# Float64 words converted in two parts in a three-layer float32 kernel: the last sum of a conversion issued with the next one

## The chip, the cores and the metric

The kernel runs on one core of a Trainium2 chip. The metric is the device time of one execution in microseconds (us); the kernel before takes 1666.84 us (median of three executions, 1666.79 to 1670.42). Engines: PE is TensorE (matmul), PEld its weight loads, DVE VectorE, ACT ScalarE, POOL GpSimd, SP the sync engine, whose queue issues most DMA transfers.

## The reference

The core of it, with batch 8, 8 heads, sequence 576, head size 64, 32 pack rows, d_model 512 and d_ff 2048:

```
p_packed = sm_attn(p, k, v)             # softmax attention, 32 rows per head
out = sm_attn(q, p_packed, p_packed)    # 576 rows per head
x = out.transpose(0, 2, 1, 3).reshape(4608, 512)
h = x @ moe_w_in;  x = (h * cos(h)) @ moe_w_out
h = x @ moe2_w_in; g = P(h) / (Q(h) + 1e-6); out = g @ moe2_w_out
```

All is float32, but the four weight matrices arrive as float64 (their scale factors make them so): each weight is two 32-bit words, and the kernel turns the words into float32 itself.

## The kernel before

Every product of the two layers is made of three float32r matmuls of split values (hi and lo parts, the function split, L66 and L67), so PE has three passes for each.

**Conversion of the words.** A tile `st` of 128 x 512 x 2 words (512 KB) is loaded; tiles of the tag st64 have three buffers. assemble does, on one tile: ACT scales the low words in place (L80); DVE shifts the high words (L82), puts sign and exponent together (L87) and cuts out the exponent (L90); POOL multiplies the low part by it (L91), which ends the use of `st`; DVE adds the two (L94). cvf and cvp are its two scratch tiles, with two buffers each. For w_out and the second layer's weights convert then makes hi on ACT (L99) and lo on POOL (L100). There are 16 conversions of moe_w_in (only the sum, into w1i), 16 of moe_w_out and 32 of the second layer's weights.

**Stage 1** (about 0 to 140 us): a loop over 16 pairs of batch and half of the heads computes the packed attention: scores (s), Exp, transposes (et), values (pv), the masked and scaled result ppm (DVE, L257), its transpose (pt). One conversion is issued by conv_next in each turn, and the load of the words three conversions on. From the fifth turn, units of the product of packed values and w_in are made (wunit: PE `w`, evacuated by ACT at L298 or DVE at L296 into wev, and written to HBM, L299).

**Stage 2** (about 140 to 840 us): 128 slots, each with mm_h (PE `h`, L532), a chain that makes g = h cos(h) (chain1: ACT u L557, DVE r L558, ACT Abs L562 and Sin L563, DVE g L564, then gh and gl by split) and mm_y of an earlier slot (PE `y`, L581). In the first nine slots `h` has one buffer, and fill puts wunits between. wq tiles are loaded from HBM (L459) and split (L66, L67). Conversions 17 to 32 are issued in the first eight slots; from slot 16 on, each three slots load (load_w2), convert (conv_w2) and write out (L478, L479) one tile of the second layer's weights.

**Stage 3** (the rest): the second layer, mm_h2, chain2 and mm_o.

The program is written in this order, but a scheduler of the language reorders each engine's instructions by its own estimate when it builds the kernel. hold only ties an instruction behind a given matmul in that order. Each engine then runs its list strictly in order.

Of the kernel before, what the change touches and what calls it, by code (L numbers as in the profile page):

```python
# [9 lines left out]
F32 = mybir.dt.float32  # L10
F32R = mybir.dt.float32r
U32 = mybir.dt.uint32
AF = mybir.ActivationFunctionType
ALU = mybir.AluOpType
# [6 lines left out]
def pack_attention_moe_moe_kernel(  # L21
# [14 lines left out]
    nc = tc.nc  # L36
# [5 lines left out]
    NG = B * G  # L42
    C = S // 32
    HS = S // 2
    NFC = DFF // 128
# [8 lines left out]
    def hold(ins, until):  # L54
        if until is None:
            return
        tc.add_manual_dep(
            ins.ins,
            until.ins.name,
            mybir.DependencyInfo(mybir.DependencyClass.NoSync, mybir.DependencyReason.SCHED_ONLY),  # L60
            reason="issue order",
        )
# [8 lines left out]
    def words(w):  # L71
        return w.bitcast(U32).rearrange("p (n t) -> p n t", t=2)

    def assemble(out, wd64, pool, n, until=None):
        up, dn = wd64[:, :, 1], wd64[:, :, 0]
        f = pool.tile([128, n], U32, tag="cvf", bufs=2, name="cvf")
        pw = pool.tile([128, n], U32, tag="cvp", bufs=2, name="cvp")
        dl = dn.bitcast(F32)
        ff, pf = f.bitcast(F32), pw.bitcast(F32)
        hold(nc.scalar.activation(out=dl, in_=dn, func=AF.Copy, scale=2.0 ** -52), until)  # L80
        hold(
            nc.vector.tensor_scalar(  # L82
                out=f, in0=up, scalar1=3, scalar2=0x3FFFFFFF, op0=ALU.logical_shift_left, op1=ALU.bitwise_and
            ),
            until,
        )
        nc.vector.scalar_tensor_tensor(  # L87
            out=f, in0=up, scalar=0xC0000000, in1=f, op0=ALU.bitwise_and, op1=ALU.bitwise_or
        )
        nc.vector.tensor_scalar(out=pw, in0=f, scalar1=0xFF800000, scalar2=None, op0=ALU.bitwise_and)  # L90
        nc.gpsimd.tensor_tensor(out=pf, in0=dl, in1=pf, op=ALU.mult)  # L91
        if out is None:
            out = ff
        nc.vector.tensor_tensor(out=out, in0=ff, in1=pf, op=ALU.add)  # L94
        return out

    def convert(hi, lo, wd64, pool, n, until=None):
        ff = assemble(None, wd64, pool, n, until)
        nc.scalar.activation(out=hi, in_=ff, func=AF.Copy)  # L99
        nc.gpsimd.tensor_tensor(out=lo, in0=ff, in1=hi.bitcast(F32), op=ALU.subtract)  # L100

    const = ctx.enter_context(tc.tile_pool(name="const", bufs=1))
    dram = ctx.enter_context(tc.tile_pool(name="scratch", bufs=1, space=DRAM))
# [5 lines left out]
    w2d = [dram.tile([2 * NFC, 128, 512], F32, name=f"w2d{i}") for i in range(2)]  # L109
# [9 lines left out]
    if True:  # L119
# [4 lines left out]
        cv_p = ctx.enter_context(tc.tile_pool(name="cv", bufs=1, side="right"))  # L124
# [24 lines left out]
        def load_kv(n):  # L149
# [10 lines left out]
            out=coef[:, 4:6], in0=par[:, 4:6], scalar1=-1.0, scalar2=None, op0=ALU.mult  # L160
# [16 lines left out]
        for n0, n1 in ((0, 2), (2, NG)):  # L177
            for h in range(4):
                nc.vector.transpose(
                    out=pbd[32 * h:32 * h + 32, n0:n1, :, h],  # L180
                    in_=px[32 * h:32 * h + 32, n0:n1].rearrange("p n (e i) -> p n e i", e=NDB),
# [28 lines left out]
        def s1(n):  # L210
            ps = ps0.tile([128, 2, 512], F32, tag="s1", bufs=2, name="s1")
            scores(ps, pbd[:, n].rearrange("p e h m -> p e (h m)"), kT_t.pop(n))
            mx = wk.tile([128, 1], F32, tag="mx", bufs=2, name="mx")
            nc.vector.tensor_reduce(out=mx, in_=ps[:, :, 0:HS], op=ALU.max, axis=AX.XY)
            nb = wk.tile([128, 1], F32, tag="nb", bufs=2, name="nb")
            nc.vector.tensor_scalar(out=nb, in0=mx, scalar1=-scale, scalar2=None, op0=ALU.mult)
            E = wk.tile([128, 6, 96], F32, tag="E", bufs=2, name="E")
            sm = wk.tile([128, 1], F32, tag="sm", bufs=2, name="sm")
            nc.scalar.activation(
                out=E.rearrange("p (t r) x -> p t (r x)", t=2),  # L220
                in_=ps[:, :, 0:HS], func=AF.Exp, scale=scale, bias=nb, accum_out=sm,
            )
            rd = wk.tile([128, 1], F32, tag="rd", bufs=3, name="rd")
            nc.vector.tensor_scalar(out=sm, in0=sm, scalar1=1e-9, scalar2=None, op0=ALU.add)
            nc.vector.reciprocal(out=rd, in_=sm)
            E_t[n], rd_t[n] = E, rd
# [134 lines left out]
        st_t = {}  # L361
# [10 lines left out]
        cv1 = [(fq, hp) for fq in range(NQ) for hp in range(NKD)]  # L372
        w1i_t, w1o_s = {}, {}
# [5 lines left out]
        def conv_w1i(x):  # L379
            fq, hp = cv1[x]  # L380
            if hp == 0:
                pool, tag, bufs = (wi_p, "w1i", 2) if fq < 2 else (wb_p, "wb", 8)
                w1i_t[fq] = pool.tile([128, NKD, 512], F32, tag=tag, bufs=bufs, name="w1i")
            assemble(w1i_t[fq][:, hp], st_t.pop(("i", x)), cv_p, 512)

        def load_w1o(f):
            load_st(f, words(w1o[128 * f:128 * f + 128, :]), nc.sync)
# [1 line left out]
        def conv_w1o(f):  # L389
            if f % 4 == 0:  # L390
                w1o_s[f // 4] = [wb_p.tile([128, 4, DM], F32R, tag="wb", bufs=8, name="w1o") for x in range(2)]
            hi, lo = w1o_s[f // 4]
            convert(hi[:, f % 4], lo[:, f % 4], st_t.pop(f), cv_p, 512)


        cvs = [(load_w1i, conv_w1i, x) for x in range(len(cv1))]
        cvs += [(load_w1o, conv_w1o, f) for f in range(NFC)]
        at_cv = [0]

        def conv_next():  # L400
            i = at_cv[0]
            at_cv[0] += 1
            if i < len(cvs):
                cvs[i][1](cvs[i][2])
            if i + 3 < len(cvs):
                cvs[i + 3][0](cvs[i + 3][2])

        prep(0)
        for i in range(3):
# [6 lines left out]
        done0 = [0]  # L416
        s1(0)
        prep(1)
        for n in range(NG + 1):
            if n >= 3:  # L420
                next(at, 1)
            if n + 1 < NG:
                s1(n + 1)
            if n + 3 < NG:
                load_k(n + 3)
            if n + 2 < NG:
                load_v(n + 2)
                prep(n + 2)
            if n < NG:
                et(n)  # L430
            if n >= 1:
                pv(n - 1)
            if n < len(cv1):
                conv_next()
            if n >= 1:
                ppt(n - 1)
            while n >= 5 and done0[0] + 1 < at_cv[0] and (n >= NG or done0[0] < 2 * (n - 4)):
                ps = ps0.tile([128, 2, 512], F32, tag="s1", bufs=2, name="w")
                for i in range(2):
                    fq, hp = cv1[done0[0]]  # L440
                    wunit(0, fq, hp, ps[:, i], False, nc.scalar)
                    done0[0] += 1
# [19 lines left out]
        def split_wq(b, j, eng, until=None):  # L462
            t = wq_t[b, j]
            split(t[:, :, 0, :], t[:, :, 1, :], t[:, :, 1, :].bitcast(F32), eng, until)
# [7 lines left out]
            hold(load_st(("w2", i), src, nc.sync), last_h[0])  # L472

        def conv_w2(i):
            hi = at_p.tile([128, 512], F32R, tag="cvh", bufs=1, name="cvh")
            lo = at_p.tile([128, 512], F32R, tag="cvl", bufs=1, name="cvl")
            convert(hi, lo, st_t.pop(("w2", i)), cv_p, 512, last_h[0])
            nc.sync.dma_start(out=w2d[0][i], in_=hi.bitcast(F32))  # L478
            nc.sync.dma_start(out=w2d[1][i], in_=lo.bitcast(F32))  # L479


        NB = NT // 512
# [38 lines left out]
        last_h = [None]  # L521
# [88 lines left out]
        def slot(n):  # L610
            nonlocal at
            b, hf, j = slots[n]
            s = hf * 8 + j
            mm_h(n)
            chain1(n)
            fill(2)
            if n >= 2:
                mm_y(n - 2)
            else:
                fill(2)  # L620
            fill(1)
            i2, ph2 = divmod(n - 16, 3)
            if 0 <= i2 < 2 * NFC:
                if ph2 == 0:
                    load_w2(i2)
                elif ph2 == 2:
                    conv_w2(i2)
            if b + 1 < B:
                if s == (0 if b else LATE):
                    at = attn2_steps(b + 1, at_p, h_tile, {"aT": ("qT", 1)}, lambda: last_h[0])  # L630
                if s % 2 == 1 if b else s >= LATE:
                    next(at, 1)
                if s == 15:
                    for _ in at:
                        pass
                for jj, (sl, ss) in enumerate(((2, 7), (10, 13), (12, 15), (14, 16))):
                    if s == sl:
                        load_wq(b + 1, jj)
                    if s == ss:
                        split_wq(b + 1, jj, nc.vector, last_h[0])  # L640
            if b > 0 and s == 0:
                split_wq(b, 3, nc.vector, last_h[0])
            move_in(n)
# [20 lines left out]
        for n in range(len(slots)):  # L664
            if n == LATE:
                fill(len(units))
                e0.close()
                at_p = e1t.enter_context(tc.tile_pool(name="at", bufs=1, side="right", **RW))
# [151 lines left out]
```

## Time and profile before

| what | value |
|---|---|
| time, median of 3 | 1666.84 us |
| time of the profiled execution | 1671.62 us |
| its span | 1669.4 us |
| PE busy in the span | 1588.6 us (95%) |
| DVE busy | 1310.0 us (78%) |
| ACT busy | 1190.8 us (71%) |
| POOL busy | 162.1 us (10%) |

The shares are means over stages with different limits, so the stages are read one by one. The 2.2 us between span and time lie around the instructions. Idle time of PE inside the span is what a change of order can win; PE's own work is the same in every order.

### The profile page before, as it was taken

How to read it: one execution, taken by the hardware profiler on the slowest of the kernel's cores; microseconds unless marked ns; L12 is line 12 of the kernel's file. 1: busy time of each engine (PE TensorE's matmuls, PEld its weight loads, DVE VectorE, ACT ScalarE, POOL GpSimd, SP SyncE). 2: the span in 40 equal slices, each digit the busy share in tenths (PEclk: the TensorE clock that was granted, in tenths of full speed). 3: DMA queues.
4: the chain of work that ended last, by engine and by line, in shares of the span. 5: the costliest groups of instructions: out<-in, count | busy, mean ns of one | idle time of the engine just before them, and what ended most of it. 6: DMA issues, size and time to landing. Idle time of an engine off the chain costs nothing.

```text
span 1669.4 us, 24912 instructions
## 1 busy us (share of the span) xinstructions
PE 1588.6 (95%) x9344; PEld 1367.7 (82%) x9344; DVE 1310.0 (78%) x2030; ACT 1190.8 (71%) x1925; POOL 162.1 (10%) x124
## 2 busy tenths in 40 slices
PE   5877999999999999999999999999999999999996
PEld 3554668999999999999998888888888888888884
DVE  7798647787878797868468888888888888888884
ACT  3357656686768686867667878777777777787874
POOL 3135300111121121211000000000000000000000
PEclk9799999999999999999999999999999999999998
DMA  9998452444444453445392201010101001020100
GB/s 281 283 318 279 154 196 88 138 141 138 136 152 141 136 162 122 143 128 160 99 310 77 65 12 53 24 51 26 51 26 44 33 13 64 1 76 1 47 5 26
DMA packets 104376, 183.56 MB, mean 110 GB/s; under 512 B 12096, under 2 KB 46912, under 8 KB 104256
## 3 DMA queue, kind: packets, MB, share of 16 engines
q1 hardware_dynamic: 97344, 167.29, 31.7%
q10 hardware_dynamic: 6912, 14.68, 2.7%
q8 instruction: 74, 1.21, 0.3%
q14 instruction: 46, 0.38, 0.1%
HBM read 117.97 MB, written 63.96 MB: 109 GB/s over the span
## 4 chain that ended last, share of the span: by engine, by line
PE 80%; DVE 6%; ACT 4%; issue 1%; DMA 1%; POOL 0%; SPq 0%; ACTq 0%; DVEq 0%; POOLq 0%
PE h L700 24%; PE o L758 23%; PE y L581 19%; PE h L532 10%; PE w L288 2%; PE s L200 2%; DVE g L564 1%; DVE r L558 1%; DVE gl L67 1%; ACT r L562 1%; DVE wq L67 1%; ACT r L563 1%; ACT L563 0%; DVE sT L350 0%; ACT u L557 0%
## 5 line engine op out<-in xcount | busy, mean ns | idle before, releaser
L581 PE MATMUL y<-gh,w1o 128*128 128x288 f32 x2048 | 438.8, 300 | 2.9 <-DVE yl L67 2.7
L700 PE MATMUL h<-x,w 128*128 128x512 f32 x1728 | 422.2, 393 | 0.0
L700 PEld LDWEIGHTS h<-x,w 128*128 128x128 f32 x1728 | 324.2, 188 | 74.2
L581 PEld LDWEIGHTS y<-gh,w1o 128*128 128x128 f32 x2048 | 338.1, 190 | 10.2 <-issue 5.3
L758 PE MATMUL o<-w,g2h 128*128 128x512 f32 x1152 | 332.9, 393 | 1.2 <-ACT g2h L718 1.2
L581 PE MATMUL y<-gl,w1o 128*128 128x288 f32 x1024 | 300.4, 299 | 2.6 <-DVE gl L67 2.4
L758 PEld LDWEIGHTS o<-w,g2h 128*128 128x128 f32 x1152 | 216.1, 188 | 51.1 <-ACT g2h L718 2.1
L532 PE MATMUL h<-ah,wq 128*128 128x288 f32 x1024 | 231.2, 301 | 11.6 <-DVE g L564 6.1
L581 PEld LDWEIGHTS y<-gl,w1o 128*128 128x128 f32 x1024 | 194.7, 190 | 6.7 <-DVE gl L67 4.2
L758 PE MATMUL o<-w,g2l 128*128 128x512 f32 x576 | 199.9, 393 | 0.0
L733 ACT ACTIVATE sq<-h 128x512 f32<-128x512 f32 x144 | 87.1, 605 | 155.7 <-PE h L700 155.6
L532 PEld LDWEIGHTS h<-ah,wq 128*128 128x128 f32 x1024 | 171.7, 189 | 19.7 <-issue 9.2
L735 DVE SCALAR_TENSOR_TENSOR ab<-sq,coef,ab 128x512 f32<-128x512 f32 x144 | 108.1, 751 | 66.7 <-ACT ab L734 66.5
L557 ACT ACTIVATE u<-h,coef 128x576 f32<-128x576 f32 x128 | 94.3, 737 | 90.1 <-PE h L532 89.6
L532 PE MATMUL h<-al,wq 128*128 128x288 f32 x512 | 151.2, 295 | 0.0
L564 DVE SCALAR_TENSOR_TENSOR g<-h,r 128x576 f32<-128x576 f32 x128 | 96.1, 753 | 59.3 <-ACT r L563 58.6
L91 POOL TENSOR_TENSOR cvp<-st,cvp 128x512 f32<-128x512 f32 x64 | 89.8, 1404 | 502.9 <-DVE cvp L90 233.9
L744 DVE SCALAR_TENSOR_TENSOR ab<-ab,y 128x512 f32<-128x512 f32 x144 | 99.4, 691 | 48.3 <-ACT y L741 48.3
L558 DVE SCALAR_TENSOR_TENSOR r<-u,h 128x576 f32<-128x576 f32 x128 | 95.3, 747 | 52.2 <-ACT u L557 51.7
L758 PEld LDWEIGHTS o<-w,g2l 128*128 128x128 f32 x576 | 108.2, 188 | 24.7
L67 DVE TENSOR_TENSOR gl<-g,gh 128x576 fp32r<-128x576 f32 x128 | 103.3, 809 | 22.3 <-ACT gh L66 21.2
L736 ACT ACTIVATE c<-h,coef 128x512 f32<-128x512 f32 x144 | 113.7, 789 | 8.7 <-DVE g2l L724 8.7
(86 smaller groups left out, 2394.1 us busy)
## 6 DMA issues: line engine op xcount, KB each, us to landing
x<-yd SPq DMA_DIRECT2D x36, 512.0 KB
w<-w2d SPq DMA_DIRECT2D x68, 256.0 KB
st<-in_moe_w_out_dram SPq DMA_DIRECT2D x32, 512.0 KB
wq<-wd SPq DMA_DIRECT2D x64, 256.0 KB
wd<-wev SPq DMA_DIRECT2D x48, 256.0 KB
kx<-in_k_dram SPq DMA_DIRECT2D x16, 576.0 KB
vx<-in_v_dram SPq DMA_DIRECT2D x48, 192.0 KB
qx<-in_q_dram SPq DMA_DIRECT2D x16, 576.0 KB
```

Source lines behind the costliest of these rows:

```text
L67: lo_eng.tensor_tensor(out=lo, in0=src, in1=hi.bitcast(F32), op=ALU.subtract)
L91: nc.gpsimd.tensor_tensor(out=pf, in0=dl, in1=pf, op=ALU.mult)
L532: last_h[0] = nc.tensor.matmul(out=ps[:, u, 0:HS], lhsT=wq[:, g, a, o:o + 128], rhs=a_t[b, g][c][:, hf * HS:hf * HS + HS], start=(i == 0), ...
L557: nc.scalar.activation(out=u, in_=ph, func=AF.Identity, bias=coef[:, 6:7])
L558: nc.vector.scalar_tensor_tensor(out=r, in0=u, scalar=RND, in1=ph, op0=ALU.subtract, op1=ALU.subtract)
L564: nc.vector.scalar_tensor_tensor(out=gt, in0=ph, scalar=2.0 * math.pi, in1=r, op0=ALU.mult, op1=ALU.mult)
L581: nc.tensor.matmul(out=y_t[d][:, 0:HS], lhsT=w1o_s[f // 4][a][:, f % 4, 128 * d:128 * d + 128], rhs=gs[c][:, u], start=(f == 0 and i == 0) ...
L700: nc.tensor.matmul(out=ps, lhsT=w2_s[f][:, 0, a, 128 * kk:128 * kk + 128], rhs=x_t[t, c, kk], start=(i == 0), stop=(i == 3 * NKD - 1),)
L735: nc.vector.scalar_tensor_tensor(out=ab, in0=sq, scalar=coef[:, 5:6], in1=ab, op0=ALU.mult, op1=ALU.add)
L736: nc.scalar.activation(out=c1, in_=ph, func=AF.Identity, scale=coef[:, 3:4], bias=coef[:, 2:3])
L744: nc.vector.scalar_tensor_tensor(out=ab, in0=ab, scalar=QC, in1=y0, op0=ALU.add, op1=ALU.mult)
L758: nc.tensor.matmul(out=o_t[s], lhsT=g2_t[n][a][:, 128 * s:128 * s + 128], rhs=w2_s[f][:, 1, c], start=(f == 0 and i == 0), stop=(f == NFC ...
```

## The change

assemble and convert become words_in (all up to the product on POOL) and words_out (DVE's sum, then hi and lo). conv_next issues words_in of conversion i, then words_out of conversion i - 1, then the load of the words of conversion i + 2 (before: i + 3). In stage 1 it is called in the seventeenth turn as well. conv_w2 leaves its words_out to the next slot with a load, right behind that load. The number of instructions of each kind is the same on every engine. The core of the diff:

```diff
-    def assemble(out, wd64, pool, n, until=None):
+    def words_in(wd64, pool, n, until=None):
...
-        nc.gpsimd.tensor_tensor(out=pf, in0=dl, in1=pf, op=ALU.mult)
-        if out is None:
-            out = ff
-        nc.vector.tensor_tensor(out=out, in0=ff, in1=pf, op=ALU.add)
-        return out
-
-    def convert(hi, lo, wd64, pool, n, until=None):
-        ff = assemble(None, wd64, pool, n, until)
-        nc.scalar.activation(out=hi, in_=ff, func=AF.Copy)
-        nc.gpsimd.tensor_tensor(out=lo, in0=ff, in1=hi.bitcast(F32), op=ALU.subtract)
+        nc.gpsimd.tensor_tensor(out=pw.bitcast(F32), in0=dl, in1=pw.bitcast(F32), op=ALU.mult)
+        return f.bitcast(F32), pw.bitcast(F32)
+
+    def words_out(fp, out=None, hi=None, lo=None, until=None):
+        f, pf = fp
+        out = f if out is None else out
+        hold(nc.vector.tensor_tensor(out=out, in0=f, in1=pf, op=ALU.add), until)
+        if hi is not None:
+            nc.scalar.activation(out=hi, in_=out, func=AF.Copy)
+            nc.gpsimd.tensor_tensor(out=lo, in0=out, in1=hi.bitcast(F32), op=ALU.subtract)
...
+        rest = [None]
+
         def conv_next():
             i = at_cv[0]
             at_cv[0] += 1
-            if i < len(cvs):
-                cvs[i][1](cvs[i][2])
-            if i + 3 < len(cvs):
-                cvs[i + 3][0](cvs[i + 3][2])
+            last, rest[0] = rest[0], cvs[i][1](cvs[i][2]) if i < len(cvs) else None
+            if last is not None:
+                last()
+            if 0 < i < len(cvs) - 2:
+                cvs[i + 2][0](cvs[i + 2][2])
...
-            if n < len(cv1):
-                conv_next()
+            conv_next()
...
-            while n >= 5 and done0[0] + 1 < at_cv[0] and (n >= NG or done0[0] < 2 * (n - 4)):
+            while n >= 5 and done0[0] + 2 < at_cv[0] and (n >= NG or done0[0] < 2 * (n - 4)):
...
+            if 0 < i2 <= 2 * NFC and ph2 == 0:
+                rest[0]()
```

What it moves, at three places on DVE. (In the changed file L82 is L81, L87 is L86, L90 is L89, L94 is L96, L296 is L295, L558 is L566, L564 is L572; cvf<-st is the start of a conversion, cvp its exponent, cvf<-cvf,cvp its sum.)

Place one, DVE around the first split of a wq tile in stage 2, from the 24th conversion's start to the first slot's r; before:

```order
L82 TENSOR_SCALAR cvf<-st_1690 128x512
L87 SCALAR_TENSOR_TENSOR cvf<-st_1690,cvf 128x512
L90 TENSOR_SCALAR cvp<-cvf 128x512
L94 TENSOR_TENSOR cvf<-cvf,cvp 128x512
L296 TENSOR_SCALAR wev<-w 128x512
L94 TENSOR_TENSOR cvf<-cvf,cvp 128x512
L67 TENSOR_TENSOR wq<-wq 128x2x512
L82 TENSOR_SCALAR cvf<-st_1702 128x512
L87 SCALAR_TENSOR_TENSOR cvf<-st_1702,cvf 128x512
L67 TENSOR_TENSOR wq<-wq 128x2x512
L90 TENSOR_SCALAR cvp<-cvf 128x512
L558 SCALAR_TENSOR_TENSOR r<-u,h 128x576
```

And the same stretch now:

```order
L81 TENSOR_SCALAR cvf<-st_1697 128x512
L86 SCALAR_TENSOR_TENSOR cvf<-st_1697,cvf 128x512
L89 TENSOR_SCALAR cvp<-cvf 128x512
L81 TENSOR_SCALAR cvf<-st_1709 128x512
L295 TENSOR_SCALAR wev<-w 128x512
L86 SCALAR_TENSOR_TENSOR cvf<-st_1709,cvf 128x512
L67 TENSOR_TENSOR wq<-wq 128x2x512
L96 TENSOR_TENSOR cvf<-cvf,cvp 128x512
L89 TENSOR_SCALAR cvp<-cvf 128x512
L67 TENSOR_TENSOR wq<-wq 128x2x512
L96 TENSOR_TENSOR cvf<-cvf,cvp 128x512
L566 SCALAR_TENSOR_TENSOR r<-u,h 128x576
```

The 24th conversion's sum goes from ahead of the first wq split to behind it, the start of the 25th comes ahead of the split in its place, and the 25th's sum now stands ahead of r. (The 23rd's sum, fourth above, is just ahead of the stretch now.)

Place two, DVE in the second slot, at the 27th conversion; before:

```order
L82 TENSOR_SCALAR cvf<-st_1807 128x512
L87 SCALAR_TENSOR_TENSOR cvf<-st_1807,cvf 128x512
L94 TENSOR_TENSOR cvf<-cvf,cvp 128x512
L90 TENSOR_SCALAR cvp<-cvf 128x512
L564 SCALAR_TENSOR_TENSOR g<-h,r 128x576
L94 TENSOR_TENSOR cvf<-cvf,cvp 128x512
```

And now:

```order
L86 SCALAR_TENSOR_TENSOR cvf<-st_1816,cvf 128x512
L89 TENSOR_SCALAR cvp<-cvf 128x512
L96 TENSOR_TENSOR cvf<-cvf,cvp 128x512
L572 SCALAR_TENSOR_TENSOR g<-h,r 128x576
L96 TENSOR_TENSOR cvf<-cvf,cvp 128x512
```

Two instructions instead of one stand between the 27th's exponent and its sum.

Place three, DVE in the third slot, from a wq split to g; before:

```order
L67 TENSOR_TENSOR wq<-wq 128x2x512
L87 SCALAR_TENSOR_TENSOR cvf<-st_1897,cvf 128x512
L558 SCALAR_TENSOR_TENSOR r<-u,h 128x576
L90 TENSOR_SCALAR cvp<-cvf 128x512
L82 TENSOR_SCALAR cvf<-st_1909 128x512
L87 SCALAR_TENSOR_TENSOR cvf<-st_1909,cvf 128x512
L296 TENSOR_SCALAR wev<-w 128x512
L90 TENSOR_SCALAR cvp<-cvf 128x512
L94 TENSOR_TENSOR cvf<-cvf,cvp 128x512
L564 SCALAR_TENSOR_TENSOR g<-h,r 128x576
```

And now:

```order
L67 TENSOR_TENSOR wq<-wq 128x2x512
L86 SCALAR_TENSOR_TENSOR cvf<-st_1904,cvf 128x512
L81 TENSOR_SCALAR cvf<-st_1916 128x512
L89 TENSOR_SCALAR cvp<-cvf 128x512
L566 SCALAR_TENSOR_TENSOR r<-u,h 128x576
L86 SCALAR_TENSOR_TENSOR cvf<-st_1916,cvf 128x512
L89 TENSOR_SCALAR cvp<-cvf 128x512
L96 TENSOR_TENSOR cvf<-cvf,cvp 128x512
L295 TENSOR_SCALAR wev<-w 128x512
L572 SCALAR_TENSOR_TENSOR g<-h,r 128x576
```

The evacuation wev<-w now stands behind an exponent and a sum that stood behind it.

## Rows read from the trace of the kernel before

**Rows 1.** The page: span, and busy time by engine.

```profile
span 1669.4 us, 24912 instructions
PE 1588.6 (95%) x9344; PEld 1367.7 (82%) x9344; DVE 1310.0 (78%) x2030; ACT 1190.8 (71%) x1925; POOL 162.1 (10%) x124
```

**Rows 2.** Busy time of each engine by stretch; first the columns.

```profile
core 0: us, PE busy (x) PEld busy (x) DVE busy (x) ACT busy (x) POOL busy (x), PEclk, DMA share, GB/s
104.00:180.00 76.00, 61.83 (x529) 39.87 (x530) 67.67 (x110) 51.12 (x91) 37.05 (x27) 0.96 0.87 279
180.00:300.00 120.00, 112.15 (x664) 95.02 (x663) 73.03 (x103) 74.49 (x117) 10.98 (x9) 0.97 0.43 142
300.00:800.00 500.00, 491.81 (x3600) 482.96 (x3599) 398.38 (x600) 365.47 (x554) 88.62 (x62) 1.00 0.44 139
800.00:1669.00 869.00, 853.24 (x3875) 703.74 (x3873) 687.96 (x1048) 662.89 (x1096) 0.00 (x0) 0.99 0.16 53
```

**Rows 3.** Timeline of PE: start, duration, instruction, [idle before <-what ended it].

```profile
146.70 0.53 PE L532 MATMUL h<-ah,wq 128*128 128x288 f32 x2 [1.22 <-DVE wq L67]
...
154.28 1.12 PE L288 MATMUL w<-w1i,wl 128*128 128x512 f32 x2 [2.70 <-ACT wev L298]
...
172.62 3.24 PE L288 MATMUL w<-w1i,wl 128*128 128x512 f32 x4 [2.18 <-DVE wev L296]
...
190.75 1.88 PE L288 MATMUL w<-w1i,wl 128*128 128x512 f32 x4
```

**Rows 4.** Who waited for whom, 110 to 290 us: total us, times, longest.

```profile
DVE cvf L94 <- POOL cvp L91: 6.3, 9, 1.2
```

**Rows 5.** Timeline of DVE, 136 to 173 us.

```profile
136.78 0.41 DVE L82 TENSOR_SCALAR cvf<-st 128x512 uint32<-128x512 uint32 x1
137.23 1.79 DVE L87 SCALAR_TENSOR_TENSOR cvf<-st,cvf 128x512 uint32<-128x512 uint32 x1
...
143.77 1.74 DVE L94 TENSOR_TENSOR cvf<-cvf,cvp 128x512 f32<-128x512 f32 x1 [0.59 <-POOL cvp L91]
145.43 1.21 DVE L67 TENSOR_TENSOR wq<-wq 128x1024 fp32r<-128x1024 f32 x1
...
148.11 0.69 DVE L87 SCALAR_TENSOR_TENSOR cvf<-st,cvf 128x512 uint32<-128x512 uint32 x1
...
149.86 0.42 DVE L90 TENSOR_SCALAR cvp<-cvf 128x512 uint32<-128x512 uint32 x1
...
151.73 0.69 DVE L94 TENSOR_TENSOR cvf<-cvf,cvp 128x512 f32<-128x512 f32 x1 [0.79 <-POOL cvp L91]
...
161.65 0.75 DVE L564 SCALAR_TENSOR_TENSOR g<-h,r 128x576 f32<-128x576 f32 x1
163.31 1.77 DVE L94 TENSOR_TENSOR cvf<-cvf,cvp 128x512 f32<-128x512 f32 x1 [0.90 <-POOL cvp L91]
...
171.88 0.68 DVE L296 TENSOR_SCALAR wev<-w 128x512 f32<-128x512 f32 x1
```

**Rows 6.** Timeline of POOL, 137 to 152 us.

```profile
137.21 1.27 POOL L100 TENSOR_TENSOR w1o<-cvf,w1o 128x512 fp32r<-128x512 f32 x1 [1.29 <-DVE cvf L82]
...
143.69 1.27 POOL L100 TENSOR_TENSOR w1o<-cvf,w1o 128x512 fp32r<-128x512 f32 x1
...
150.41 1.29 POOL L91 TENSOR_TENSOR cvp<-st,cvp 128x512 f32<-128x512 f32 x1 [2.62 <-issue]
```

**Rows 7.** Timeline of ACT at the first wq split of stage 2.

```profile
141.97 1.06 ACT L66 ACTIVATE wq<-wq 128x1024 fp32r<-128x1024 f32 x1 [0.69 <-DMA wq<-wd]
```

**Rows 8.** Waits of SP's DMA queue, 100 to 180 us.

```profile
SPq L368 <- POOL cvp L91: 20.2, 9, 5.5
```

**Rows 9.** Who waited for whom, 290 to 800 us.

```profile
PE h L532 <- DVE g L564: 5.2, 9, 1.1
...
PE y L581 <- DVE gl L67: 2.4, 4, 1.0
...
DVE cvf L94 <- POOL cvp L91: 2.4, 5, 0.8
```

More of the change, by code (lines that the diff above doesn't have):

```diff
@@ L78, in assemble @@
         dl = dn.bitcast(F32)
-        ff, pf = f.bitcast(F32), pw.bitcast(F32)
         hold(nc.scalar.activation(out=dl, in_=dn, func=AF.Copy, scale=2.0 ** -52), until)
@@ L383, in conv_w1i @@
                 w1i_t[fq] = pool.tile([128, NKD, 512], F32, tag=tag, bufs=bufs, name="w1i")
-            assemble(w1i_t[fq][:, hp], st_t.pop(("i", x)), cv_p, 512)
+            fp = words_in(st_t.pop(("i", x)), cv_p, 512)
+            return lambda: words_out(fp, out=w1i_t[fq][:, hp])
         def load_w1o(f):
@@ L392, in conv_w1o @@
             hi, lo = w1o_s[f // 4]
-            convert(hi[:, f % 4], lo[:, f % 4], st_t.pop(f), cv_p, 512)
+            fp = words_in(st_t.pop(f), cv_p, 512)
+            return lambda: words_out(fp, hi=hi[:, f % 4], lo=lo[:, f % 4])
         cvs = [(load_w1i, conv_w1i, x) for x in range(len(cv1))]
@@ L474, in conv_w2, with fin @@
         def conv_w2(i):
[L475 to L479, printed above, removed]
+            fp = words_in(st_t.pop(("w2", i)), cv_p, 512, last_h[0])
+            def fin():
+                hi = at_p.tile([128, 512], F32R, tag="cvh", bufs=1, name="cvh")
+                lo = at_p.tile([128, 512], F32R, tag="cvl", bufs=1, name="cvl")
+                words_out(fp, hi=hi, lo=lo, until=last_h[0])
+                nc.sync.dma_start(out=w2d[0][i], in_=hi.bitcast(F32))
+                nc.sync.dma_start(out=w2d[1][i], in_=lo.bitcast(F32))
+            rest[0] = fin
         NB = NT // 512
```

## The prediction

> **What bounds the kernel now.** I read the page first, then busy time by stretch, then PE's timeline with its gaps, and only then the waits of DVE, POOL and SP. The page gives PE 1588.6 of 1669.4 us busy [rows 1], so nothing that leaves PE's work alone can win more than PE's gaps. The stretches say where these lie [rows 2]: from 300 to 800 us PE lacks 8.2 of 500 us, from 180 to 300 us 7.9 of 120, and from 104 to 180 us 14.2 of 76. No conversion is left after 800 us (POOL busy 0.00 there), and DVE's list is unchanged up to the 16th conversion's exponent, just ahead of 104 us. So the change acts in two stretches: the busy one at 104 to 180 us, where DVE is 67.67 of 76 us busy, and the long one to 800 us, where PE is nearly full.
>
> The target of the change is a wait on DVE: the sum of a conversion stands close behind its exponent, and POOL's product lies between them. From 110 to 290 us DVE sat idle for it nine times, 6.3 us together [rows 4]; from 290 to 800 us five times, 2.4 us [rows 9].
>
> **Instructions and loads.** No instruction is added or removed on any engine, so PE's, ACT's and POOL's own time is as before: 0 us. The loads now stand two conversions ahead in the program, not three, but the words still have three buffers, so a load still waits for the product of the conversion three back. SP's list has the same four word loads ahead of the first wq loads. SP's wait for that product, 20.2 us in nine waits from 100 to 180 us [rows 8], therefore stays unless the product itself comes earlier. I take 0 for the loads.
>
> **Why the 6.3 us are not simply won.** While POOL works, DVE's next step often can't. The step L87 takes 0.69 us alone, but 1.79 us where it started 0.02 us behind a POOL instruction of 1.27 us [rows 5, 6]: it ended at 139.02, POOL's at 138.48, so it ran its own 0.5 to 0.7 us after POOL was done. The sums themselves show the same, 1.74 us beside POOL's L100 at 143.69 and 0.69 us alone. If the wait is taken away and L82 or L87 of the next conversion stands there, that instruction meets the same product. The rows make the value per moved sum nearer 0 than its whole wait.
>
> The Trainium skill says the same more strongly (SBUF — State Buffer, section "Who interferes with whom"): VectorE and GpSimd share one pair of ports under an exclusive lock, and the second to issue fully blocks. By that rule none of the 6.3 us comes back where a step with two SBUF inputs follows; without it all would. The rows at 137.2 us agree with it.
>
> **Place one, the first wq split.** PE waited 1.22 us for it [rows 3]. Its input from ACT was ready at 141.97 + 1.06 = 143.03, and DVE reached it at 145.43, behind a sum with 0.59 us of waiting and 1.74 us of run [rows 5, 7]. That sum, 2.33 us, goes behind the split; L82 and L87 of the next conversion, 0.41 + 0.69 = 1.10 us, come ahead. Split earlier by 1.2 us. Up to the first slot's r two sums are added behind it (2 x 0.69) and those 1.10 us are gone: 0.3 us back. The second of these sums has only the other wq split, 1.21 us, between its exponent and itself, while a product takes 1.29 us or more [rows 5, 6]: some 0.4 us of new wait with the semaphores. Left: 1.2 - 0.3 - 0.4 = 0.5 us won. Bounds: 2.4 us won (145.43 - 143.03) and 0.7 us lost (0.3 + 0.4 with no earlier split).
>
> **Place two, the second slot.** The wait of 0.90 us at 163.31 [rows 5] had g (0.75 us) alone between exponent and sum; now a sum and g stand there, 0.69 + 0.75 = 1.44 us, over a product's 1.29. I take 0.8 us won, between 0 (the steps between are blocked as above) and 0.9, because g took its plain 0.75 us at 161.65 with that same product under way behind it.
>
> **Place three, the third slot.** PE waited 2.18 us for the evacuation on DVE (L296) at 171.88 [rows 3, 5]. An exponent and a sum, 0.42 + 0.69 = 1.11 us, now stand ahead of it, and behind it on DVE is only g, which comes at the same time as before. PE has nothing else there: 1.1 us lost, between 0 (if place two and the earlier start cover it) and 1.1 + 1.3 us (if the product is not done).
>
> **290 to 800 us.** The sum moves to the next slot in the program, but the scheduler had already put 1 to 6 other instructions between exponent and sum, and now puts 2 to 9. PE's waits there are for g and gl, 5.2 + 2.4 us [rows 9], in slots where ACT's Sin or the attention's long DVE steps are late, and the five waits at a sum are 2.4 us of a DVE that is 80% busy. I take 0, between 2.4 us won and as much lost by another order.
>
> **Sum.** -0.5 - 0.8 + 1.1 = -0.2 us. The profiled execution took 1671.62 us (its span and 2.2 us around it), so it would become 1671.4. That execution is 4.8 us above the median of 1666.84, so against the median I forecast 1666.6 us. A change under 0.3%, 5.0 us, can't be told from none here.
>
> **The rivals.**
>
> *The waits were on the path.* DVE is the busiest engine from 104 to 180 us, and each sum that ends sooner lets the next conversion, the product and the load behind it come sooner, so that SP's 20.2 us shrink too. For it: those waits hold up wq splits, ppm and evacuations that PE waits for. Against it: POOL's 37.05 us in those 76 us [rows 2] block DVE's next step as well. It gives 1666.84 - 6.3 = 1660.5 us; with the 2.4 us of the later stretch 1658.1.
>
> *Sums in front of a slot's work.* At places one and three a sum now stands ahead of r and of wev. If the product is not ready when DVE gets there, the whole slot waits: 1.29 + 0.69 = 2.0 us at each, 4.0 us, and the exponent's 0.4 at place three. After such a gap PE's next four matmuls took 3.24 us where they take 1.88 us in a full stretch [rows 3], 1.4 us more. Together 5.8 us: 1672.6 us. It decides from the point where the instructions between exponent and sum take less than the product; at place one these are 1.21 us against 1.29. Against it: at place three five instructions stand between.
>
> *The change does not do what it says.* The scheduler writes each engine's order by its own estimate and had already parted most sums from their exponents, so that the new program gives nearly the old schedule: 1666.8 us.
>
> **How the numbers follow.** The forecast gets 0.50, the unchanged schedule 0.14 (both are no difference that can be told: 0.64), the waits on the path 0.20 (faster), the sums in front 0.16 (slower). The range takes in most of the two outer cases: from 1660.5, the first rival's time, to 1671.9, just short of the second rival and of the forecast with every bound at its worst (0.7 + 2.4 + 2.4 = 5.5 us lost, 1672.3). The forecast's own range is 1662 to 1671.
>
> **What would show it.** Right: DVE's wait for POOL at the sum falls from 6.3 us to some 2 to 4 us before 290 us, steps L86 and L81 of over 1.5 us become more frequent, and PE's busy time by stretch stays within 2 us. Place one right: PE's wait for the first wq split under 1 us; place three right: PE's wait for wev at about 172 us near 3 us. Wrong: PE's gaps from 104 to 180 us fall under 10 us (first rival) or rise over 18 us (second), or PE's 8.2 us from 300 to 800 us change by more than 3.

## The result, and the profile after

The changed kernel takes **1679.11 us** (median of six executions, 1674.12 to 1683.33) where the kernel before takes 1667.8 in the same comparison (six, 1666.55 to 1672.89): ratio **1.0063, with an interval of 1.0041 to 1.0084**. By this ratio it is slower by some 10.5 us. The prediction said 1666.6, between 1660.5 and 1671.9, and gave "slower" 0.16: it was wrong, and the time lies outside its range.

One pair of traces shows 7.5 of these us: the profiled execution of before, at 1671.62 us, is itself 3.8 us above its median, that of the change within 0.4 us of its own. The experiments show where the rest lies.

The change's profiled execution took 1678.78 us. The page's first rows, to be held against [rows 1]:

```profile
span 1676.9 us, 24917 instructions
PE 1587.9 (95%) x9344; PEld 1367.9 (82%) x9344; DVE 1314.3 (78%) x2030; ACT 1189.7 (71%) x1925; POOL 160.4 (10%) x124
```

PE worked as long as before (1587.9 and 1588.6 us) in a span that is 7.5 us longer, so on the whole the loss is idle time of PE. Busy time by stretch, with the columns of [rows 2]:

```profile
104.00:180.00 76.00, 60.30 (x530) 39.31 (x530) 65.45 (x106) 49.35 (x90) 36.25 (x26) 0.98 0.87 267
180.00:300.00 120.00, 110.32 (x639) 92.91 (x638) 71.91 (x103) 74.33 (x116) 10.92 (x8) 0.96 0.44 142
300.00:800.00 500.00, 488.49 (x3559) 479.23 (x3559) 401.93 (x597) 361.79 (x548) 86.47 (x62) 1.00 0.44 139
```

From 104 to 180 us, where the prediction placed all its terms, PE did the same 530 matmuls in 76 us as before (529). What it is short of lies behind: 639 matmuls instead of 664 in the second stretch, 3559 instead of 3600 in the third. To see where, I took the start of the first `h` matmul of each of the 128 slots out of both traces. A difference that grows between two slots was lost between them (us, change minus before):

```
slot        0     1     2     3     4    16    60    72   108   112   127
before  143.8 154.8 162.6 174.9 183.9 274.5 505.6 567.2 752.3 772.6 844.3
change  -2.48 +0.72 +0.07 -0.47 -0.09 -0.12 +1.33 +5.72 +5.48 +7.18 +7.48
```

In this pair nothing is lost or won up to slot 16; more executions of the same lists tell otherwise, as the experiments show. Then come three steps: 1.5 us soon behind slot 16, 4.4 us between slots 60 and 72, 1.7 us between slots 108 and 112. PE's timeline names the gaps; first the change (the first three rows answer to [rows 3]):

```profile
144.28 0.53 PE L540 MATMUL h<-ah,wq 128*128 128x288 f32 x2 [0.26 <-DVE wq L67]
150.52 5.54 PE L287 MATMUL w<-w1i,wl 128*128 128x512 f32 x8 [3.80 <-ACT wev L297]
172.97 1.98 PE L287 MATMUL w<-w1i,wl 128*128 128x512 f32 x4 [2.72 <-DVE wev L295]
...
288.60 0.58 PE L540 MATMUL h<-ah,wq 128*128 128x288 f32 x1 [2.80 <-DVE g L572]
...
519.32 0.37 PE L540 MATMUL h<-ah,wq 128*128 128x288 f32 x1 [2.08 <-DVE g L572]
549.38 0.40 PE L589 MATMUL y<-gh,w1o 128*128 128x288 f32 x1 [1.28 <-DVE yl L67]
...
770.15 0.37 PE L540 MATMUL h<-ah,wq 128*128 128x288 f32 x1 [2.07 <-DVE g L572]
```

And the same matmuls of the kernel before (at 549 us there was no gap):

```profile
286.95 0.37 PE L532 MATMUL h<-ah,wq 128*128 128x288 f32 x1 [0.87 <-DVE g L564]
...
516.30 0.37 PE L532 MATMUL h<-ah,wq 128*128 128x288 f32 x1 [0.26 <-DVE g L564]
...
762.99 0.37 PE L532 MATMUL h<-ah,wq 128*128 128x288 f32 x1 [0.26 <-DVE g L564]
```

Each gap at `h` is a wait for g, the instruction that frees the tile of `h` which the next slot needs. Behind two of them the granted clock fell as well. Windows of 8 us that hold the end of each gap for g, in the change (columns as in [rows 2]):

```profile
286.00:294.00 8.00, 5.40 (x31) 5.43 (x31) 7.08 (x15) 5.45 (x11) 0.00 (x0) 0.79 0.69 211
518.00:526.00 8.00, 6.68 (x39) 6.71 (x40) 7.48 (x12) 6.49 (x10) 1.32 (x1) 0.79 0.13 51
768.00:776.00 8.00, 5.93 (x45) 5.88 (x45) 7.89 (x14) 6.07 (x9) 0.49 (x1) 1.00 0.39 129
```

A mean of 0.79 over 8 us stands for some 3.4 us at the lower level, 1.2 GHz. What such a fall costs can be read from the slots: the change lost 3.22 us from slot 60 to slot 64, with the clock down, and 1.70 from slot 108 to 112, with the clock up, behind gaps of the same size; in e7 (below) it was 1.71 with the clock up at the first and 3.21 with the clock down at the second. So a fall costs 1.5 us. Before, the clock was at 1.00 in the windows around all three. So the step behind slot 16 is a gap that grew by 1.9 us and up to 1.5 us of clock (a part of the fall lies inside the gap), of which some 2 us come back by slot 60 (before's waits of 0.68 us at 298 us and 1.04 us at 344 us are gone); the one behind slot 60 is 1.8 us of gap, 1.5 of clock and 1.3 of a wait for yl, 0.2 more than the step; the last is 1.8 us of gap alone. That yl had itself waited on DVE, until an earlier yl was written to HBM:

```profile
548.87 0.46 DVE L67 TENSOR_TENSOR yl<-y,yh 128x288 fp32r<-128x288 f32 x1 [2.71 <-DMA yd<-yl]
```

**Why g is late at 288 us.** Here is ACT in the kernel before, from the u's of slots 16 and 17 to slot 16's Sin, from which its g follows:

```profile
282.43 0.74 ACT L557 ACTIVATE u<-h,coef 128x576 f32<-128x576 f32 x1 [4.11 <-PE h L532]
283.48 0.74 ACT L557 ACTIVATE u<-h,coef 128x576 f32<-128x576 f32 x1 [0.30 <-PE h L532]
284.12 0.67 ACT L562 ACTIVATE r<-r 128x576 f32<-128x576 f32 x1
284.94 0.41 ACT L66 ACTIVATE yh<-y 128x288 fp32r<-128x288 f32 x1
285.25 0.77 ACT L563 ACTIVATE r<-r,coef 128x576 f32<-128x576 f32 x1
```

And in the changed one:

```profile
284.52 0.74 ACT L565 ACTIVATE u<-h,coef 128x576 f32<-128x576 f32 x1 [0.31 <-PE h L540]
285.16 0.70 ACT L66 ACTIVATE yh<-y 128x288 fp32r<-128x288 f32 x2
285.74 1.27 ACT L570 ACTIVATE r<-r 128x576 f32<-128x576 f32 x2
286.88 1.45 ACT L571 ACTIVATE r<-r,coef 128x576 f32<-128x576 f32 x2
```

Two copies of yh and both Abs now stand ahead of the first Sin: from the second u's start to that Sin 1.77 us before (285.25 - 283.48), 2.36 now, 0.6 us more. The u's themselves come 1.04 us later, because PE's list has other `y` matmuls ahead of the `h` that they read. No conversion is in any of these rows: the scheduler wrote another order.

**Why g is late at 519 us.** DVE before, and POOL's lo of the conversion that runs there:

```profile
513.00 1.21 DVE L67 TENSOR_TENSOR wq<-wq 128x1024 fp32r<-128x1024 f32 x1
514.14 0.75 DVE L67 TENSOR_TENSOR al<-aT,ah 128x576 fp32r<-128x576 f32 x1
514.81 0.68 DVE L94 TENSOR_TENSOR cvf<-cvf,cvp 128x512 f32<-128x512 f32 x1
515.41 0.74 DVE L564 SCALAR_TENSOR_TENSOR g<-h,r 128x576 f32<-128x576 f32 x1
...
516.23 1.30 POOL L100 TENSOR_TENSOR cvl<-cvf,cvh 128x512 fp32r<-128x512 f32 x1 [3.77 <-DVE g L564]
```

And now:

```profile
512.94 0.67 DVE L96 TENSOR_TENSOR cvf<-cvf,cvp 128x512 f32<-128x512 f32 x1
...
514.20 1.22 DVE L67 TENSOR_TENSOR wq<-wq 128x1024 fp32r<-128x1024 f32 x1
515.33 1.85 DVE L67 TENSOR_TENSOR al<-aT,ah 128x576 fp32r<-128x576 f32 x1
517.10 0.74 DVE L566 SCALAR_TENSOR_TENSOR r<-u,h 128x576 f32<-128x576 f32 x1
517.77 0.76 DVE L353 STREAM_TRANSPOSE aT<-sT 128x576 f32<-128x576 f32 x1
518.46 0.71 DVE L572 SCALAR_TENSOR_TENSOR g<-h,r 128x576 f32<-128x576 f32 x1
...
515.10 1.47 POOL L99 TENSOR_TENSOR cvl<-cvf,cvh 128x512 fp32r<-128x512 f32 x1 [2.63 <-ACT cvh L98]
```

From the wq split's start to g it was 2.41 us, now it is 4.26. The 1.85 more are r (0.67 to the next start) and aT (0.69), which stand ahead of g, and al, which is lengthened by 1.10 because POOL's lo now runs beside it; the sum, which has gone forward, gives back 0.60. So here the moved sum has a share: POOL's product began at 511.15 us in both, the sum came at 514.81 before and comes at 512.94 now, and with it POOL's lo at 515.10, where al is. The gap at 770 us has the same rows: from 765.02 us the wq split, al of 1.85 us beside a lo of POOL, r, aT and g follow one another as here, 4.27 us from the split's start to g.

The targets of the change did get smaller. DVE's waits for POOL at the sum (110 to 290 us) and SP's wait for the product (100 to 180 us), to be held against [rows 4] and [rows 8], and PE's wait for g (290 to 800 us) against [rows 9]:

```profile
DVE cvf L96 <- POOL cvp L90: 3.6, 5, 1.2
...
SPq L367 <- POOL cvp L90: 17.7, 8, 5.3
...
PE h L540 <- DVE g L572: 6.6, 8, 2.1
```

### The profile page after: what moved, and what is told of

Same layout as the page of the kernel before. It is cut to its first block, busy times and chain, and to the rows that moved or that the text cites. A ratio compares the mean times of both kernels' runs of the same rounds, so it can differ in the third digit from the quotient of the medians.

```text
span 1676.9 us, 24917 instructions
## 1 busy us (share of the span) xinstructions
PE 1587.9 (95%) x9344; PEld 1367.9 (82%) x9344; DVE 1314.3 (78%) x2030; ACT 1189.7 (71%) x1925; POOL 160.4 (10%) x124
## 4 chain that ended last, share of the span: by engine, by line
PE 79%; DVE 7%; DMA 6%; ACT 4%; issue 2%; POOL 1%; SPq 0%; ACTq 0%; POOLq 0%; DVEq 0%
PE h L710 24%; PE o L768 23%; PE y L589 18%; PE h L540 10%; DMA vx<-in_v_dram 2%; PE s L199 2%; PE w L287 2%; DVE g L572 1%; DVE r L566 1%; DMA wd<-wev 1%; DMA st<-in_moe_w_out_dram 1%; DMA px<-in_p_dram 1%; ACT r L570 1%; ACT r L571 1%; DMA qx<-in_q_dram 1%
## 5 line engine op out<-in xcount | busy, mean ns | idle before, releaser
L572 DVE SCALAR_TENSOR_TENSOR g<-h,r 128x576 f32<-128x576 f32 x128 | 95.5, 752 | 62.7 <-ACT r L571 61.8
L566 DVE SCALAR_TENSOR_TENSOR r<-u,h 128x576 f32<-128x576 f32 x128 | 95.2, 746 | 53.3 <-ACT u L565 53.1
L90 POOL TENSOR_TENSOR cvp<-st,cvp 128x512 f32<-128x512 f32 x64 | 89.6, 1401 | 488.9 <-DVE cvp L89 214.7
```

The lines of the kernel that those rows point to most:

```text
L90: nc.gpsimd.tensor_tensor(out=pw.bitcast(F32), in0=dl, in1=pw.bitcast(F32), op=ALU.mult)
L566: nc.vector.scalar_tensor_tensor(out=r, in0=u, scalar=RND, in1=ph, op0=ALU.subtract, op1=ALU.subtract)
L572: nc.vector.scalar_tensor_tensor(out=gt, in0=ph, scalar=2.0 * math.pi, in1=r, op0=ALU.mult, op1=ALU.mult)
```

## The experiments

Each kernel's medians and intervals are against executions of the kernel before on the same chip, in turn with it. For the profiled execution of each the slots' starts stand below, minus before's (us). The same lists give other times ahead of slot 16 (the change itself: -0.12, and +1.04 in e4; e7 and e8, which have its lists up to there, +5.27 and -0.01). So what a kernel loses is read from slot 16 on, row "from 16".

All the same, the two groups differ ahead of slot 16. Four other executions have before's lists up to slot 15, and reach it 1.8 to 2.4 us sooner than before's profiled execution did (e2, e6, e9, and e10 with -2.38): that one was late by itself. Six have the change's lists up to there (the change, e4, e1, e5, e7, e8) and reach it between 0.1 us sooner and 5.3 us later. The medians of the two groups are -1.8 and +2.4 us. So, as far as eleven executions tell, the change loses some 2 to 7 us there as well, about 4 between the medians, and the first pair of traces hid it.

```
slot      e1     e2     e3     e4     e5     e6     e7     e8     e9    e10
4      +3.64  -1.62  -1.68  +1.05  +2.59  -1.76  +3.41  -0.14  -1.49  -2.20
16     +3.66  -1.82  +1.80  +1.04  +4.46  -1.88  +5.27  -0.01  -1.78  -3.76
60     +5.69  +0.19  +3.64  +2.79  +5.84  -0.09  +6.04  +0.88  -0.82  -5.17
72     +5.71  +4.39  +3.66  +6.83  +5.84  -0.07  +9.16  +2.96  +0.51  -5.16
127    +6.21  +6.20  +4.26  +8.50  +6.48  +0.15 +12.04  +4.13  +0.57  -5.12
from 16 +2.6   +8.0   +2.5   +7.5   +2.0   +2.0   +6.8   +4.1   +2.4   -1.4
```

### One half of the change at a time, and the change again

**e1**: the first layer's conversions as in the change (deferred sums, the call in the seventeenth turn), the second layer's whole.

```diff
-            fp = words_in(st_t.pop(("w2", i)), cv_p, 512, last_h[0])
-            def fin():
...
-                words_out(fp, hi=hi, lo=lo, until=last_h[0])
...
+            words_out(words_in(st_t.pop(("w2", i)), cv_p, 512, last_h[0]), hi=hi, lo=lo)
```

> Only conv_next is divided (with its call in the seventeenth turn and the later units); the second layer's conversions are whole, as before. Scheduler theory (the loss is another order of stage 2, not the parting itself): the same steps at slots 16 to 20 as in the change, h of slot 20 about 1.7 us later than before, and a time 2 to 6 us over before. Deferral theory (the sums that wait for the next slot are late): all sums of conv_next are done by 205 us and h of slot 16 was not late in the change, so 0 us, within 1.5 us of before.

Measured: 1675.39 us against 1670.77, ratio 1.0029 (1.0019 to 1.0039).

**e2**: the reverse, only the second layer's sum deferred; conv_next as before.

```diff
-                cvs[i][1](cvs[i][2])
+                cvs[i][1](cvs[i][2])()
```

> Only the second layer's conversions are divided, their sum tied behind the next slot's matmul; conv_next is as before. Deferral theory: the whole loss, 8 to 11 us over before, with PE's gaps of some 2 us at h near 519 and 770 us and a gap at yl near 549 us as in the change. Scheduler theory: no step at slots 16 to 20 (within 0.3 us of before there), a part of the loss later, 2 to 6 us over before.

Measured: 1677.6 us, ratio 1.0038 (1.0023 to 1.0054). There is no step at slot 20. From slot 20 to slot 48 e2 loses 2.4 us at a place of its own, a gap for g that was 1.04 us before, with the clock down behind it (0.79 from 338 to 346 us):

```profile
340.66 0.38 PE L540 MATMUL h<-ah,wq 128*128 128x288 f32 x1 [1.83 <-DVE g L572]
```

The gap at 519 us is there too, with its clock (0.68 us for two matmuls is the lower level, 0.43 the upper):

```profile
518.19 0.38 PE L540 MATMUL h<-ah,wq 128*128 128x288 f32 x1 [2.08 <-DVE g L572]
...
519.12 0.68 PE L540 MATMUL h<-ah,wq 128*128 128x288 f32 x2
```

**e3**: the kernel before with conv_next called in the seventeenth turn too. Nothing is deferred and no load moved.

```diff
-            if n < len(cv1):
-                conv_next()
+            conv_next()
```

> The kernel before with one difference: conv_next is also called in the seventeenth turn of stage 1, so each later conversion is issued one call earlier. Nothing is divided, no load is moved, no sum deferred. Scheduler theory: the order of stage 2 from slot 16 on changes as in the change, h of slot 20 some 1.7 us late, 2 to 6 us over before. Deferral theory: 0 us, within 1.5 us of before.

Measured: 1675.83 us, ratio 1.0034 (1.0021 to 1.0048).

**e4**: the change once more. 

> The change once more, beside the others on the same chip. Both theories: 8 to 11 us over before. If the loss is partly a clock that falls behind PE's gaps of over 2 us, executions differ by about 1.7 us steps, and the trace shows one 3.4 us stretch at half clock behind one, two or three of the gaps at h near 288, 519 and 770 us.

Measured: 1680.4 us, ratio 1.0065 (1.0050 to 1.0081), with the gaps of the first profile (2.80, 2.08, 0.92 and 2.08 us).

What follows: by the medians the halves add up (0.0029 + 0.0038 against 0.0065); by the slots they do so only in part. From slot 60 to slot 127 e2 loses 6.0 us and e1 0.5, the change 6.2 and e4 5.7: what is lost there is the second half's. From slot 16 to slot 60 e1 and e2 lose 2.0 us each, at different places, but the change 1.5 and e4 1.8. The first half's loss needs no deferral, for e3, which defers nothing, loses as much. What e1 and e3 share is the order from slot 16 on, but for a few rows, with PE's 2.79 us wait for g in each:

```profile
289.16 0.58 PE L531 MATMUL h<-ah,wq 128*128 128x288 f32 x1 [2.79 <-DVE g L563]
```

Two more programs need no run. With the loads two conversions ahead and nothing else, every engine's list is row for row that of the kernel before; so the loads' distance moves nothing. And the change without the tie of the second layer's sum (until=last_h[0] in fin) gives the lists of e1 on every engine: the scheduler puts that sum back where it was, and only the tie behind the next slot's matmul moves it.

### The order, without the change

**e5**: the first layer's sums deferred, but no conversion shifted by a call; the second layer whole.

```diff
-            conv_next()
+            if n < len(cv1):
+                conv_next()
+            else:
+                rest[0]()
+                rest[0] = None
```

> The sums of the first layer's conversions issued with the next conversion, as in the change, but with no conversion shifted by a call (stage 1 issues its last sum by itself in the seventeenth turn) and the second layer's conversions whole. Theory of the order (the loss lies in the order of ACT and DVE at slots 16 to 18, where ACT now copies two yh ahead of Abs and Sin): that order stands here too, so PE waits some 2.8 us for g at about 288 us, the clock falls behind it, and from slot 16 to the end 2 to 4 us are lost; in all 2 to 6 us above the kernel before, ratio 1.0015 to 1.0035. Rival (the shift by a call is what costs): ratio 0.999 to 1.001.

Measured: 1674.12 us against 1670.87, ratio 1.0022 (1.0008 to 1.0037), and the same wait of 2.80 us, at 293.15 us. The rival (the shift costs) falls: either edit alone turns the order at slot 16, and each then loses 2.0 to 2.6 us behind it. The lists of e5 are, row for row on every engine, those of e1: once the sums are deferred, the call in the seventeenth turn moves nothing, and e5 is in effect e1 measured again (1.0022 and 1.0029).

**e6**: the kernel before, with two yh copies put ahead of both Abs at slots 16 and 17 by ties, and nothing else.

```diff
-                    split(yh, yl, y_t[d][:, 0:HS], nc.vector)
+                    yhc = split(yh, yl, y_t[d][:, 0:HS], nc.vector)
+                    if n == 15 and d == 1:
+                        hold(abs_t[16], yhc)
+                        hold(abs_t[17], yhc)
```

> The kernel before, nothing of the change in it; in one place, slots 16 and 17, two of the four yh copies of ACT are tied ahead of both Abs, as the change's order has them. Theory of the order: up to slot 16 as before (within 0.5 us, or one run's drift), then the gap of 0.87 us for g at 287 us becomes some 2.8 us, with a stretch at half clock behind it: from slot 16 to the end 2 to 3.5 us lost, ratio 1.0012 to 1.0021. Rival (conversions under way at that time are what costs): 0, ratio 0.9995 to 1.0005.

Measured: PE's gap for g goes from 0.87 to 2.40 us, with the clock behind it:

```profile
286.61 0.37 PE L535 MATMUL h<-ah,wq 128*128 128x288 f32 x1 [2.40 <-DVE g L567]
...
286.00:294.00 8.00, 7.39 (x44) 7.42 (x45) 7.82 (x14) 5.01 (x10) 1.32 (x1) 0.79 0.70 208
```

From slot 16 on 2.0 us are lost, the low end of what was expected, and about as much as in e3 and e5. The tie turns rows of the lists up to slot 51, but 1.9 of the 2.0 us are lost by slot 20. The executions give 1671.8 us against 1670.87, ratio 1.0008 (0.9996 to 1.0020): 2 us lie inside that interval, and so does nothing. The trace shows the loss; the time alone would not.

**e7**: the change, with slot 17's yh copies tied behind that slot's Sin.

```diff
-                    split(yh, yl, y_t[d][:, 0:HS], nc.vector)
+                    split(yh, yl, y_t[d][:, 0:HS], nc.vector, last_sin[0] if n == 15 else None)
```

> The change, with the four yh copies of slot 17 tied behind that slot's Sin. Theory of the order: g comes some 1.5 us sooner, PE's gap at 288 us falls from 2.8 to about 1.3 us; if the half clock behind it goes too, 3.2 us are won, if not 1.5: ratio to the kernel before 1.0045 to 1.0057 instead of 1.0065; the gaps at 519 and 770 us stay at 2.1 us. Rival: PE waits as long for something else, ratio 1.006 to 1.007.

Measured: 1679.67 us, ratio 1.0053 (1.0035 to 1.0072); no difference from e4 can be told by the time. From slot 16 to slot 20 e7 lost 1.1 us where e4 lost 2.1. The gap fell by 1.0 us, not 1.5, and a new wait came behind it:

```profile
292.94 0.37 PE L541 MATMUL h<-ah,wq 128*128 128x288 f32 x1 [1.77 <-DVE g L573]
299.23 0.40 PE L590 MATMUL y<-gl,w1o 128*128 128x288 f32 x1 [0.88 <-DVE gl L67]
...
772.00:780.00 8.00, 6.43 (x37) 6.46 (x38) 7.48 (x13) 6.36 (x10) 1.05 (x1) 0.79 0.28 88
```

The expectation was too high: it left out that u, too, comes 1.04 us later in the change's list of PE (0.87 + 1.04 is close to the 1.77 left). The clock stayed up at 292 and 524 us, and fell behind the gap at 773 us, where it had not in the change's first profile.

### The later place, at slot 60

**e8**: the change, with the last transposes of batch 4's attention (aT) tied behind the slot's g.

```diff
-                nc.vector.transpose(out=aT, in_=sT[:, g])
+                hold(nc.vector.transpose(out=aT, in_=sT[:, g]), late() if b == 4 else None)
```

> The change, with the last transposes of the attention of batch 4 (DVE aT, slots 61 to 64) tied behind that slot's g. Theory of the order: PE's gap of 2.1 us for g at 519 us falls under 0.7 us and the half clock behind it goes: 2.5 to 3.5 us won, ratio to the kernel before 1.0043 to 1.0050 instead of 1.0065; the gaps at 288 and 770 us stay. Rival (DVE has too much to do there, in any order): the wait goes to ah or al of slot 64 with the same 2 us, ratio 1.006 to 1.007.

Measured: 1678.68 us, ratio 1.0050 (1.0031 to 1.0069). The gap at 519 us is gone and its clock with it, and so is the wait for yl; but a gap of 3.11 us has come for g at slot 66:

```profile
538.70 0.37 PE L541 MATMUL h<-ah,wq 128*128 128x288 f32 x1 [3.11 <-DVE g L573]
```

Between slots 60 and 72 the kernel lost 2.1 us (0.88 to 2.96) where e4 lost 4.0: 2 us won of 2.5 to 3.5 expected. Both theories were partly right: the order made that gap, and a tie which mends one slot moves the work to another.

**e9**: the kernel before, with r and aT put ahead of g in slot 60, as the change has them. All other lists stay as they were up to there.

```diff
+                if b == 4 and g == 1:
+                    hold(g_t[60], aTi)
+                    hold(g_t[60], r_t[61])
```

> The kernel before, nothing of the change in it; in one place, slot 60, DVE's g is tied behind the second aT of batch 4 (0.77 us) and slot 61's r (0.71 us), as the change's order has them; all else stands as before up to there. Theory of the order: PE's gap for g at 516 us grows from 0.26 us by some 1.4 to about 1.6 us, nothing later wins it back: 1.4 us lost, or 3.1 if the clock falls behind the gap; slots 68 to 127 later by 1.2 to 3.2 us than slot 60, ratio 1.0006 to 1.002. Rival (the sum's own work, or POOL beside DVE, is what costs there): under 0.4 us, ratio 0.9996 to 1.0004. The lengthened al (1.85 us instead of 0.75) is the change's alone, so this cannot show the whole 2.1 us gap.

Measured: the gap grows from 0.26 to 1.58 us, as worked out:

```profile
514.59 0.77 DVE L355 STREAM_TRANSPOSE aT<-sT 128x576 f32<-128x576 f32 x1
515.29 0.71 DVE L562 SCALAR_TENSOR_TENSOR r<-u,h 128x576 f32<-128x576 f32 x1
515.93 0.74 DVE L568 SCALAR_TENSOR_TENSOR g<-h,r 128x576 f32<-128x576 f32 x1
...
516.81 0.37 PE L536 MATMUL h<-ah,wq 128*128 128x288 f32 x1 [1.58 <-DVE g L568]
```

From slot 60 to slot 72 it loses 1.33 us and never wins them back; the clock stayed up. (1.0 of the 2.4 us in the table's last row lie at slot 17, where the lists are before's.) 1671.84 us against 1669.73, ratio 1.0009 (0.9998 to 1.0019): again too little for the time alone.

### A version with the order mended elsewhere

**e10**: the kernel before, with ties that bring batch 1's first aT and ah ahead of slot 15's r and of the wq split beside them.

```diff
+                if b == 1 and g == 0:
+                    hold(r_t[15], aTi)
...
-                        split_wq(b + 1, jj, nc.vector, last_h[0])
+                        split_wq(b + 1, jj, nc.vector, first_ah[0] if b == 0 and jj == 2 else last_h[0])
```

> The kernel before with ties of its own at slot 16: the sums and scaling of batch 1's attention, its first aT and ah come ahead of slot 15's r and of the wq split beside them; aimed at the gap of 2.59 us for ah at 274 us, the largest that is left in stage 2 after 250 us. Theory of the order: ah ends some 1.6 us sooner, so slot 16 starts 1.2 to 2 us sooner; slots 17 to 20 may lose up to 1 us of it by their new order; if the clock no longer falls behind that gap, 1.7 us more: ratio 0.9980 to 0.9995. Rival (g of slots 14 and 15, which free the tiles of h, ends that wait as late as ah): 0, ratio 0.9995 to 1.001.

Measured: the gap of 2.59 us for ah at 274 us becomes 1.20 us for g, and the clock no longer falls there (1.00 from 250 to 300 us, 0.97 before):

```profile
270.69 0.37 PE L540 MATMUL h<-ah,wq 128*128 128x288 f32 x1 [1.20 <-DVE g L572]
```

Slot 127 starts 2.7 us sooner than slot 15 would have it (-5.12 against -2.38). In time it is 1669.36 us against 1669.73, ratio 0.9995 (0.9986 to 1.0003): clearly faster than the change, not told apart from the kernel before. No version that surely beats both was found.

## Why the prediction was wrong, step by step

- **Instructions and loads, 0 us: right.** PE's busy time differs by 0.7 us in 1588, and the loads' distance alone leaves every list as it was.
- **The waits are not simply won: right.** DVE's wait fell from 6.3 to 3.6 us, within the 2 to 4 forecast, and none of it reached the end. Steps beside POOL were lengthened, the wq split at 145.44 us to 2.33 us and al at 515.33 us to 1.85. The Trainium skill (SBUF — State Buffer, section "Who interferes with whom") says that VectorE and GpSimd share one pair of ports under an exclusive lock; these rows agree with it. One sign did not come: steps L86 and L81 of over 1.5 us were not more frequent (four from 110 to 290 us, five before).
- **Place one, -0.5 us: nothing was won.** The wait for the first split did fall, from 1.22 to 0.26 us (0.70 to 1.22 in the five executions of before's lists ahead of slot 15, 0.25 to 0.54 in the six of the change's). But the 0.4 us put down for a new wait of the second sum was something else: that sum did not wait, the wq split ahead of it was lengthened beside POOL. And the term lacked what came next: PE's wait for wev grew from 2.70 to 3.80 us, because ACT's evacuation waited until an earlier wev was written to HBM:

```profile
145.44 2.33 DVE L67 TENSOR_TENSOR wq<-wq 128x1024 fp32r<-128x1024 f32 x1 [0.28 <-ACT wq L66]
...
149.87 0.60 ACT L297 ACTIVATE wev<-w 128x512 f32<-128x512 f32 x1 [3.23 <-DMA wd<-wev]
```

  From slot 0 to slot 2 the six take 20.4 to 21.3 us and the five 18.8 to 20.0; two more `w` matmuls, 1.0 us, lie in the six.
- **Places two and three, -0.8 and +1.1 us.** Of place two's wait of 0.90 us, 0.52 us stayed. Place three was right: the gap for wev in the third slot is 2.46 to 2.73 us in the six and 1.00 to 1.35 in e2, e6, e9 and e10, 1.3 us more; before's 2.18 was the longest of its five. (Between exponent and sum there stand three instructions, not the five that the prediction counts.)
- **The sum of the three places, -0.2 us: this step failed as well.** That the first pair of traces gives -0.12 at slot 16 is chance, for before's execution was late there by itself. Between the groups some 4 us are lost ahead of slot 16. Place three has 1.3 of them; for the rest no row is shown here, and its cause stays open.
- **"290 to 800 us ... I take 0, between 2.4 us won and as much lost by another order": this step failed.** From slot 16 on 7.6 us are lost, three times the bound, and PE lacks 11.5 us from 300 to 800 us where it lacked 8.2, a sign that the prediction itself had named for being wrong. It priced the waits that the sums had there, 2.4 us, and took that sum as the bound for the order too. But the order that changed is that of the slots' own chains, u, r, Abs, Sin, g. At 288 us no conversion stands in it; at 519 and 770 us one takes part, with 1.10 us by which POOL's lo lengthens al. Its first place, 287 us, was not in the term at all. The bound should have come from what stands ahead of g: one Abs and one yh more on ACT (0.6 us), r and aT on DVE (1.4), al beside POOL (1.1), with an h tile waiting, and 1.5 us of clock behind a gap. Three such places, with the wait for yl at 549 us, give the loss from slot 16 on.
- **The rivals.** "Sums in front of a slot's work" forecast 1672.6 us at places one and three. At place three a sum and an exponent did cost 1.3 us; at place one PE waited for the write of wev, not for a sum. Its kind (something ahead of what PE waits for, and the clock behind the gap) was what happened from slot 16 on, with r, aT and yh in the place of the sums. "It does not do what it says" held for one part: untied, the second layer's sum went back to its place. "The waits were on the path" found no support: the waits shrank and PE gained nothing.

What is shown: either edit of the first half turns the order at slot 16; e6 makes that gap in the kernel before, without the change. e9 does the same for 1.32 of the 1.82 us by which the gap at 519 us grew; the 0.50 left are al's 1.10 less the sum's 0.60. The loss behind slot 60 is the second half's (e2). What stays open: why PE's own list at slot 17 puts u 1.04 us later; the wait for yl at 549 us; the gap at 770 us, which comes 48 slots behind the one at 519 us with the same rows, but was not tried by itself; and the loss ahead of slot 16.

## What to carry to other kernels

Where a scheduler writes the lists, an edit's cost is not only in the instructions it moves: hold the lists of before and after against each other in every stage, above all the chain that frees the tile the bottleneck waits for, and count what newly stands ahead of its last steps. A stretch in which the bottleneck is 98% busy has little to win from a removed wait and 2 us to lose at each such place. And compare two traces by the start of the same step of the loop: it tells in which slot time is lost, where busy shares and sums of waits hide it. Do it with several executions of each: one pair hid some 4 us here.

## What had not been expected of the hardware

The same gap brings the clock down in one execution and not in another. In the change's profile it fell to 1.2 GHz behind the gap of 2.08 us at 519 us and not behind that of 2.07 at 770; in e7 it was the other way round (1.00 from 522 to 530 us, 0.79 from 772 to 780). It did not fall behind e8's 3.11 us, and fell behind e6's 2.40. Where its cost can be read, a fall took some 1.5 us, not much less than the gap itself. And the same lists reached slot 16 up to 5.4 us apart in six executions (-0.12, +1.04, +3.66, +4.46, +5.27 and -0.01): effects of 1 to 2 us were seen here only from a slot on, not in whole times.
